# FFN 1's first projection as seven block products per pair of tiles, for tiles 8 to 15 of 18

## The chip, the cores and the metric

One core of one Trainium2 chip runs the whole program. The metric is the device time of one execution in microseconds (us). TensorE (PE) multiplies, VectorE (DVE), ScalarE (ACT) and GpSimd (POOL) do the elementwise work, SyncE (SP) issues nearly all DMAs. Only PE, DVE and ACT reach PSUM here, which has eight banks of 128 x 512 float32.

## The reference

Sliding-window attention with a linear bias, then two feed-forward networks (FFNs) on the same 2304 tokens of 512 numbers:

```python
scores = scale * q @ k.T + bias          # 4 batches, 8 heads, 576 positions, head size 64, window 128
x = softmax(scores) @ v                  # -> 2304 x 512
# FFN 1
h = x @ w_in                             # 512 -> 1024
solu = h * softmax(h)
ln = (solu - mean(solu)) / sqrt(var(solu) + 1e-6) * g_ln
x = ln @ w_out                           # 1024 -> 512
# FFN 2
g = x @ w_gate                           # 512 -> 1536
y = (silu(g) * (x @ w_val)) @ w_out2     # 1536 -> 512
```

## The kernel before

**Numbers.** PE works on a rounded 32-bit form (F32R). A float32 operand is split into a high and a low half (`high`, line 270, and `low`, line 276), and a product is taken as three matmuls, high x low, low x high and high x high (`HALVES`). The weights arrive as 64-bit words; `fetch` loads them and `unpack` (lines 311 to 319) turns them into float32 on ACT, DVE and POOL before they are split.

**Attention** goes in 20 steps (4 batches of five query tiles, the fifth half as long), each of four pairs of heads: `score` (line 463, matmuls on 32 x 64 pieces of the array), maximum and bias on DVE (499, 504), the exponential on ACT with the row sum as a second output (530, 539), then the transpose of the weights on PE (558), its copies out of PSUM (568 DVE, 571 ACT) and the product with v (607). In the first `SUMS` steps the division by the row sum is made after the product, with the inverted sums spread over a PSUM bank by matmuls (615, tile `rs` in SBUF holds the sums). In the later steps the sum goes to a PSUM bank, DVE inverts it (509, 510), and DVE, ACT or POOL divide (515, 517). The result is split into the halves of one token tile (128 tokens), in one of three places (`xs_at`).

**FFN 1** goes over 18 token tiles. `up(i)` is the first projection: two PSUM banks, 12 matmuls of 512 columns for each (line 712 in `pieces`), 24 for a tile; then maximum (735), exponential (746), product with h (748), variance (754), the power -0.5 on POOL (768) and the normalization (771). `flip(i)` transposes the tile, on PE (817) or, for tiles in `FLIP_BY_DMA`, by 16-bit halves through HBM (`pl`, 263 to 265, and `lscr`). `down1(i)` is the second projection, 24 matmuls of 512 columns, also at line 712, and its result goes to HBM (849).

**FFN 2** (`products`, line 1083; `steps_of`, line 1262) multiplies 2 x 2 blocks by seven products in place of eight (the Winograd form of Strassen's method): sums of blocks are made first (`seven`, line 982), and the products are added up in PSUM and on DVE.

**The order.** Each step is a generator that asks for slots (buffers, PSUM banks) and submits operations with a rank. The planner `Emitter.run` (line 199) keeps a clock for each engine with estimated costs, and emits, wherever an engine is free, the operation of the lowest rank that is ready; where an operation may go to several engines, the sum of end time and a bias (`B_DVE`, `B_ACT`) decides. So every constant at the head of the file moves instructions in all queues. At run time each engine executes its queue strictly in that order. A change between ordinary matmuls, those on 32 x 64 pieces (`form` 1) and those on 128 x 64 pieces (`form` 2) is counted by the planner at 95 ns, and `LEAST` and `PATIENCE` say how long such work is held back to be done together.

Of the kernel before, what the change touches and what calls it, by code (L numbers as in the profile page):

```python
# [35 lines left out]
PAIRS = (9, 29)  # L36
NTAIL = 2
DEC1 = (4, 2)
DEC2 = (2, 4)
RAW = 4  # L40
# [6 lines left out]
FLIP_BY_DMA = range(4, 14)  # L47
PLB = 2
SUMS = 4
PTB = 4  # L50
WHOLE = 20
VDB = 3
PW_2 = -0.766
LEAD = 3.373
R_FLIP = 0.741
R_DOWN = 3.0
PW_IN = [-0.63, -0.31, -0.37, -0.36, 0.17, 0.09, 0.35, 0.2]
PW_OUT = 5.23
B_DVE = 1863.684
B_ACT = 700.0  # L60
HALVES = [(0, 1), (1, 0), (0, 0)]
HB = NC2 // 2
O_MAX = 0.338
O_EXP = -0.005
O_INV = 0.814
O_TURN = -0.064
O_PT = -1.188
O_VAL = 0.0
O_X = 0.674
O_SC = 0.33  # L70
O_DEC = 0.0
O_SPL = -0.05
O_FLIP = -1.299
O_LN = -0.345
O_SET = 0.102
O_FREE = -1.17
# [3 lines left out]
PATIENCE = 517.289  # L80
LEAST = 3
# [27 lines left out]
class Emitter:  # L109
# [6 lines left out]
    def __init__(self):  # L116
        self.busy, self.pending, self.count, self.open = {}, [], 0, {}
        self.now = 0.0
        self.form = 0

# [77 lines left out]

    def run(self):
        while self.pending:  # L200
# [17 lines left out]
            if engine == "PE":  # L218
                if first > TOGETHER and getattr(fn, "form", 0) != self.form:
                    cost += 95.0  # L220
                self.form = getattr(fn, "form", 0)
            self.pending.remove(op)
# [9 lines left out]
def attention_then_two_ffns(ctx: ExitStack, tc: tile.TileContext, qk, v, w_in, w_out, g_ln, w2, tables_d, out):  # L232
# [28 lines left out]
    def halves_of(dst, src, n):  # L261
        words = src.bitcast(U16).rearrange("p (c h) -> p h c", h=2)
        return [(ACT, t_act(2 * n), lambda: nc.scalar.copy(dst, words)),
                (DVEP, t_dve(2 * n), lambda: nc.vector.tensor_copy(dst, words)),
                (POOL, 450.0 + 0.3 * 2 * n, lambda: nc.gpsimd.tensor_copy(dst, words))]
# [10 lines left out]
    def low(lo, src, hi, n, sbuf=True):  # L276
# [3 lines left out]
        return ways  # L280

# [202 lines left out]
    def attend(u):  # L484
# [34 lines left out]
        if c < SUMS:  # L519
            em.give(bank_s, ds[1], k)  # L520

            if pr == 0:
                yield rs_s
                rs[c] = at.tile([P, 3, 2 * NPAIR], F32, tag="rs", bufs=3, name="rs")
# [4 lines left out]
            for j, d in enumerate(ds):  # L529
                ex.append((yield (ACT, 93 + t_act(P, True, True), lambda j=j: nc.scalar.activation(  # L530
                    e[0:n, j], e[0:n, j], AF.Exp, bias=st[0:n, j:j + 1], scale=-1.0,
                    accum_out=rs[c][0:n, 0, 2 * pr + j:2 * pr + j + 1]), [d, ds[0]], 0.0, O_EXP)))
# [61 lines left out]
        if c < SUMS and pr == NPAIR - 1:  # L594
            for r in range(NPAIR):
                yield summed[c * NPAIR + r]
            y = yield (DVE, 160, lambda: nc.vector.tensor_scalar_add(rs[c][0:n, 1], rs[c][0:n, 0], 1e-9), (), 0.0, O_INV)
            inv.append((yield (DVE, 190, lambda: nc.vector.reciprocal(rs[c][0:n, 2], rs[c][0:n, 1]), [y], 0.0, O_INV)))
            sum_of[c] = yield bank_s

        def values():
# [9 lines left out]
            if inv:  # L611
                sums = banks[sum_of[c]].rearrange("p (r q) -> p r q", r=NPAIR)
                for r in range(NPAIR):
                    for j in range(2):
                        nc.tensor.matmul(sums[j * 64:(j + 1) * 64, r, 0:n], rs[c][0:n, 2, 2 * r + j:2 * r + j + 1].to_broadcast([n, 64]),
# [30 lines left out]
        while done < n:  # L646
            i, o = divmod(t0 + done, P)
            w = min(P - o, n - done)
            if i not in x_tiles:
                x_at[i] = yield x_s  # L650
                x_tiles[i] = xs_at[x_at[i]]
            hi, lo = (y[:, :, o:o + w] for y in x_tiles[i])
            src = src_x[:, :, done:done + w]
# [53 lines left out]

    def pieces(o, terms, per, cost):
# [7 lines left out]
    def up(i):  # L716
# [7 lines left out]
        (mx, mx2, sm, sm2, su, su2, nmu, nmu32, va, va2, s1, eps, var, rr) = (st[:, j:j + 1] for j in range(14))  # L724
# [18 lines left out]
        x = yield (DVE, 205, lambda: nc.vector.tensor_scalar(mx, mx, mx2, None, ALU.min), tops)  # L743
# [24 lines left out]
        x = yield (POOL, 470, lambda: nc.gpsimd.tensor_tensor(rr, var, mhalf, ALU.pow), [x])  # L768
# [122 lines left out]
    def fair(ways):  # L891
        return [(*w, 0.0) for w in ways]

    RG = NTT + LEAD + 2.4
    PROD = {"11": (0, 0), "22": (1, 1), "a4": (2, 5), "s3": (3, 6), "s1": (4, 4), "s2": (5, 3), "s4": (6, 2)}
# [7 lines left out]
    def second_region():  # L903
        for u in range(NU):
            yield started[u]
        yield valued[NS - 1]
        esa.close()
# [468 lines left out]
```

## Time and profile before

| | |
|---|---|
| median of 3 runs | 732.59 us (730.68 to 733.17) |
| the profiled execution | 732.14 us |
| its span, first to last instruction | 730.3 us |
| PE matmul, busy | 704.8 us (97%), 5148 matmuls |
| PE weight loads, busy | 635.2 us (87%) |
| DVE, ACT, POOL, busy | 540.0, 458.1, 272.2 us |

Times in the rows are in microseconds from the first instruction, unless marked ns. A matmul's end is modelled, and matmuls overlap, so the sum of their durations is longer than the time that they take in a row; the chain of waits gives that time, since in it a piece lasts until the next one begins. "PEld" is the loading of the stationary operand. L712 is line 712 of the kernel before.

### The profile page before, as it was taken

What the parts mean: (1) busy time and instruction counts of PE and PEld (TensorE: products, weight loads), DVE (VectorE), ACT (ScalarE), POOL (GpSimd) and SP (SyncE); (2) the same over time, 40 slices, a digit from 0 to 9 for tenths busy, and PEclk for the clock granted to TensorE, in tenths of its full rate; (3) what the DMA queues carried; (4) which work ended last, traced back from release to release, by engine and by line L of the source; (5) the groups of instructions that cost most, each with busy time, mean ns of one, the idle gap of its engine ahead of it and who ended that gap; (6) DMA issues with size and microseconds to landing.
All of it is one profiled execution on the core that took longest, in us unless ns stands there. A gap on an engine that the chain in (4) does not pass through costs nothing.

```text
span 730.3 us, 14535 instructions
## 1 busy us (share of the span) xinstructions
PE 704.8 (97%) x5148; PEld 635.2 (87%) x5148; DVE 540.0 (74%) x1480; ACT 458.1 (63%) x1127; POOL 272.2 (37%) x278
## 2 busy tenths in 40 slices
PE   5899899999999999999999999999999999999998
PEld 3567678777888888888899999999999999999997
DVE  6888985476566656988978767667775599886966
ACT  7899977777667775776647555655563574442532
POOL 3777776545675563550022412424221002110200
PEclk9999999999999999999999999999999999999999
DMA  8853325524454326256443454365541798886951
GB/s 289 249 168 109 103 73 146 167 89 116 133 151 109 94 75 173 73 145 148 150 170 131 151 169 163 125 188 190 184 151 66 263 360 307 254 299 203 300 177 66
DMA packets 92297, 121.86 MB, mean 167 GB/s; under 512 B 46400, under 2 KB 58688, under 8 KB 92224
## 3 DMA queue, kind: packets, MB, share of 16 engines
q1 hardware_dynamic: 91808, 120.48, 52.2%
q8 instruction: 40, 0.66, 0.4%
q10 hardware_dynamic: 416, 0.46, 0.2%
q14 instruction: 33, 0.27, 0.1%
HBM read 76.62 MB, written 34.34 MB: 152 GB/s over the span
## 4 chain that ended last, share of the span: by engine, by line
PE 76%; ACT 10%; DVE 9%; issue 2%; DMA 1%; POOL 1%; ACTq 0%; SPq 0%; DVEq 0%; POOLq 0%
PE bank L1083 31%; PE bank L712 21%; PE bank L1262 18%; PE bank L607 2%; ACT e L539 2%; PE bank L463 2%; PE bank L558 2%; ACT bank L754 1%; ACT pt L571 1%; ACT e L530 1%; DVE e L504 1%; PE bank L817 1%; DVE yt L277 1%; DMA tables<-tables 1%; DVE pt L568 1%
## 5 line engine op out<-in xcount | busy, mean ns | idle before, releaser
L1083 PE MATMUL bank<-yt,w 128*128 128x384 f32 x1008 | 186.3, 337 | 1.8 <-ACT t L1112 1.0
L1083 PEld LDWEIGHTS bank<-yt,w 128*128 128x128 f32 x1008 | 176.2, 188 | 4.1 <-ACT set L1110 1.5
L1262 PE MATMUL bank<-w,wo 128*128 128x384 f32 x756 | 133.1, 337 | 0.6 <-DVE set L1123 0.6
L319 POOL TENSOR_TENSOR db<-db,dw 128x512 int32<-128x512 int32 x52 | 73.2, 1409 | 161.2 <-DVE db L317 110.7
L1262 PEld LDWEIGHTS bank<-w,wo 128*128 128x128 f32 x756 | 132.4, 188 | 0.9 <-DVE set L1123 0.9
L712 PE MATMUL bank<-wout,lnT 128*128 128x512 f32 x432 | 102.5, 392 | 0.0
L1083 PE MATMUL bank<-shared,w 128*128 128x384 f32 x504 | 97.6, 337 | 0.0
L712 PEld LDWEIGHTS bank<-wout,lnT 128*128 128x128 f32 x432 | 80.4, 188 | 16.7 <-issue 0.2
L1083 PEld LDWEIGHTS bank<-shared,w 128*128 128x128 f32 x504 | 88.2, 188 | 1.1 <-ACT set L1110 0.5
L712 PE MATMUL bank<-shared,shared 128*128 128x512 f32 x288 | 79.8, 410 | 0.8 <-ACT shared L273 0.8
L712 PEld LDWEIGHTS bank<-shared,shared 128*128 128x128 f32 x288 | 52.2, 191 | 13.0 <-issue 1.9
L539 ACT ACTIVATE e<-e,st 128x128 f32<-128x128 f32 (+1 forms) x128 | 49.7, 402 | 21.5 <-DVE st L504 19.8
L273 ACT CAST w<-t 128x384 fp32r<-128x384 f32 (+2 forms) x35 | 26.6, 771 | 39.7 <-DVE t L1206 27.4
L504 DVE CUSTOM_DVE_ANT_0 e<-bank,bias 128x128 f32<-128x128 f32 (+1 forms) x160 | 38.2, 283 | 6.9 <-PE bank L463 5.0
L517 POOL TENSOR_TENSOR e<-e,st 128x256 f32<-128x256 f32 (+1 forms) x55 | 33.2, 618 | 21.9 <-ACT e L539 9.9
L277 DVE TENSOR_TENSOR w<-db,w 128x512 fp32r<-128x512 f32 (+1 forms) x46 | 31.4, 690 | 12.7 <-ACT w L273 12.4
L311 ACT ACTIVATE dw<-dw 128x512 int32<-128x512 uint32 x52 | 35.0, 675 | 7.0 <-DMA dw<-w 5.1
L316 DVE TENSOR_SCALAR db<-db 128x512 uint32<-128x512 uint32 x52 | 27.5, 532 | 16.0 <-ACT db L315 16.0
L273 ACT CAST w<-db 128x512 fp32r<-128x512 f32 (+1 forms) x48 | 26.9, 566 | 19.7 <-POOL db L319 9.4
L317 DVE SCALAR_TENSOR_TENSOR db<-dw,db 128x512 uint32<-128x512 uint32 x52 | 38.5, 744 | 0.8
L712 PE MATMUL bank<-shared 128*128 128x512 f32 x144 | 39.1, 394 | 0.0
L558 PE MATMUL bank<-tables,e 128*128 128x128 f32 x160 | 29.7, 293 | 9.0 <-ACT e L530 5.8
(124 smaller groups left out, 1242.7 us busy)
## 6 DMA issues: line engine op xcount, KB each, us to landing
dw<-w SPq DMA_DIRECT2D x36, 512.0 KB, 4.1
t<-ascr SPq DMA_DIRECT2D x21, 768.0 KB, 6.0
ascr<-set SPq DMA_DIRECT2D x34, 384.0 KB, 2.7
later<-ascr SPq DMA_DIRECT2D x15, 768.0 KB, 5.9
wo<-wscr SPq DMA_DIRECT2D x6, 896.0 KB, 7.2
v<-v SPq DMA_DIRECT2D x20, 256.0 KB, 3.6
lscr<-pl SPq DMA_DIRECT2D x20, 256.0 KB, 2.4
raw<-qk SPq DMA_DIRECT2D x19, 256.0 KB, 4.0
```

The source lines that it names most:

```text
L273: return [(ACT, t_act(n, sbuf), lambda: nc.scalar.copy(hi, src)), (DVEP if sbuf else DVE, t_dve(n, sbuf), lambda: nc.vector.tensor_copy(hi ...
L277: ways = [(DVEP if sbuf else DVE, t_dve(n), lambda: nc.vector.tensor_sub(lo, src, hi.bitcast(F32)))]
L311: r = yield (ACT, t_act(512), lambda: nc.scalar.activation(a, lw, AF.Copy, scale=2.0 ** -29), (), 0.0, O_DEC)
L317: x = yield (DVEP, t_dve(512), lambda: nc.vector.scalar_tensor_tensor(b, hw, 0x80000000, b, ALU.bitwise_and, ALU.bitwise_or), [x], 0.0, O_DEC)
L319: x = yield (POOL, t_pool(512), lambda: nc.gpsimd.tensor_tensor(b.bitcast(I32), b.bitcast(I32), a, ALU.add), [x, r], 0.0, O_DEC)
L504: d = yield (DVE, t_dve(P), lambda j=j: nc.vector.tensor_tensor_reduce(e[0:n, j], sc[0:n, j * 256:j * 256 + P], bias[0:n, 2 * pr + j, bs], ...
L517: eng.tensor_tensor(e[0:n], e[0:n], st[0:n, 6:8].unsqueeze(2).to_broadcast([n, 2, P]), ALU.mult)
L539: ex.append((yield (ACT, 93 + t_act(P, True, True), lambda j=j: nc.scalar.activation(e[0:n, j], e[0:n, j], AF.Exp, bias=st[0:n, j:j + 1], ...
L558: nc.tensor.transpose(tp[:, j], e[:, j], ident)
L712: nc.tensor.matmul(o, terms[m][0], terms[m][1], start=(m == 0), stop=(m == len(terms) - 1))
L1083: nc.tensor.matmul(o, l, r, start=first and m == 0, stop=m == 5, skip_group_check=True)
L1262: nc.tensor.matmul(o, w[:, b], ob[k, i][a][:, j], start=i == 0 and m == 0, stop=i == HB - 1 and m == 2)
```

## The change

For tiles 8 to 15 the first projection of FFN 1 is made two tiles at a time (`UPP`), by seven products of 2 x 2 blocks for eight. The two rows of blocks are the two tiles; the 512 inner numbers and the 1024 columns are halved. Each product is six matmuls of 512 columns: 42 for a pair, where two tiles took 48.

- `sums_of_w` makes four sums of blocks of `w_in` once, after the last weight of `w_out` has been decoded, and puts them into the buffers of the decoder (`dw`, `db`), into `rec`, and into one new tile (`sums`).
- The attention result of these tiles is copied to `xf` as float32, not split. One `xf` holds a pair, and there is one (`XF`).
- `combine` makes the block sums of the pair with `seven` and splits them into `xc` (one set).
- `up_pair` issues the seven products (line 876 of the changed kernel) in four banks: 11, 22, s1, s2, s4, s3, a4. A bank is added to again after it has been copied out: s2 waits for the copy of 11, s4 for that of s1, s3 for that of s2 (ACT, line 881), a4 for a DVE sum.
- The row sums of the first `SUMS` steps go to a PSUM bank (taken at the start of the step) in place of SBUF; `SUMS` is 5 for 4.
- The planner counts slow stretches of PE's clock (`paced`, with `WARM` and `COOL`), and nearly all its constants have new values. Tile 3 is transposed through HBM too, and there are three `raw` tiles for four and one `pl` for two.

The diff, cut to its core:

```diff
+UPP = range(8, 16, 2)
+XF = 1
-RAW = 4
+RAW = 3
-FLIP_BY_DMA = range(4, 14)
-PLB = 2
-SUMS = 4
+FLIP_BY_DMA = range(3, 14)
+PLB = 1
+SUMS = 5
-LEAD = 3.373
-R_FLIP = 0.741
+LEAD = 3.281
+R_FLIP = 0.274
-B_DVE = 1863.684
-B_ACT = 700.0
+B_DVE = 1575.488
+B_ACT = 554.749
...
-PATIENCE = 517.289
-LEAST = 3
+PATIENCE = 134.638
+LEAST = 4
+WARM, COOL = 3400.0, 1900.0
...
+    def paced(self, t, cost):
+        gap = t - self.warmed
+        if gap > COOL:
+            self.rest = WARM
+        elif self.rest and gap > 400.0:
+            self.rest = WARM
+        slow = min(2 * cost, self.rest)
+        self.rest -= slow
+        cost += slow / 2
+        self.warmed = t + cost
+        return cost
...
-                    accum_out=rs[c][0:n, 0, 2 * pr + j:2 * pr + j + 1]), [d, ds[0]], 0.0, O_EXP)))
+                    accum_out=banks[sum_of[c]][0:n, 2 * pr + j:2 * pr + j + 1]), [d, ds[0]], 0.0, O_EXP)))
...
+    def up_pair(i):
...
+        kd = yield bank_s
+        x1 = yield from product(kd, "11", first=True)
+        c1 = yield (*copied(ei[:, 0], kd, x1)[0], *copied(ei[:, 0], kd, x1)[1:])
+        kx = yield bank_s
+        x2 = yield from product(kx, "22", first=True)
+        a1 = yield summed_(banks[kx], ei[:, 0], kx, tops[0][0], [x2, c1])
+        kb = yield bank_s
+        x5 = yield from product(kb, "s1", first=True)
+        c5 = yield (*copied(ej[:, 0], kb, x5)[0], *copied(ej[:, 0], kb, x5)[1:])
+        x6 = yield from product(kd, "s2", [c1])
+        u2 = yield (*copied(ei[:, 1], kd, x6)[0], *copied(ei[:, 1], kd, x6)[1:])
+        x3 = yield from product(kb, "s4", [c5])
+        a2 = yield summed_(banks[kb], ei[:, 1], kb, tops[0][1], [x3, u2])
+        em.start(soft(i, ei, sts[0], [kx, kb], [a1, a2], 2), i + LEAD)
+        x7 = yield from product(kd, "s3", [u2])
+        kz = yield bank_s
+        a3 = yield summed_(banks[kz], ej[:, 0], kd, tops[1][1], [x7, c5])
+        x4 = yield from product(kd, "a4", [a3])
+        a4 = yield (DVE, t_dve(512), lambda: nc.vector.reduce_max(tops[1][0], banks[kd], axis=AX.X), [x4])
+        em.give(xc_s, x4)
+        em.start(soft(i + 1, ej, sts[1], [kd, kz], [a4, a3], 2), i + 1 + LEAD)
...
+    em.start(sums_of_w(), R_T + LEAD)
     for i in range(NTT):
-        em.start(up(i), i + LEAD)
+        if i in UPP:
+            em.start(up_pair(i), i + LEAD)
+        elif i - 1 not in UPP:
+            em.start(up(i), i + LEAD)
```

Two places show how instructions move. On PE, before, the first projection of a tile stands in long runs. This is the end of tile 9 (`shared` holds `w_in` and x, `lnT` is the normalized and transposed tile of `down1`, `tables,e` is a transpose in attention):

```order
L712 MATMUL bank_83<-shared_73,shared_74 128x512 x2
L712 MATMUL bank_83<-shared_73 128x512 x4
L712 MATMUL bank_84<-shared_74,shared_73 128x512 x4
L712 MATMUL bank_84<-shared_73,shared_74 128x512 x4
L712 MATMUL bank_84<-shared_73 128x512 x4
L712 MATMUL bank_82<-wout_76,lnT_2293 128x512 x8
L712 MATMUL bank_82<-wout_75,lnT_2294 128x512 x8
L712 MATMUL bank_82<-wout_75,lnT_2293 128x512 x8
L558 MATMUL bank_80<-tables,e 128x128 x2
```

In the change, for the pair of tiles 12 and 13, the end of product s1 (bank 81), then s2 (bank 79), two transposes, s4 (bank 81 again) and s3 (bank 79 again) stand so:

```order
L876 MATMUL bank_81<-dw,xc_2126 128x512 x2
L876 MATMUL bank_79<-dw,xc_2126 128x512 x2
L876 MATMUL bank_79<-dw,xc_2127 128x512 x2
L876 MATMUL bank_79<-dw,xc_2126 128x512 x2
L580 MATMUL bank_86<-tables,e 128x128 x2
L580 MATMUL bank_83<-tables,e 128x128 x2
L876 MATMUL bank_81<-shared_74,xc_2126 128x512 x2
L876 MATMUL bank_81<-shared_73,xc_2127 128x512 x2
L876 MATMUL bank_81<-shared_73,xc_2126 128x512 x2
L876 MATMUL bank_79<-sums,xc_2126 128x512 x2
L876 MATMUL bank_79<-sums,xc_2127 128x512 x2
L876 MATMUL bank_79<-sums,xc_2126 128x512 x2
```

Where no bank was used twice by one tile, banks 81 and 79 now come back one product and two transposes later, with a copy in between on another engine.

On ACT, before, the work of an attention step stands together in the middle stretch. Here are exponentials (539), the cast of an attention result (273), two divisions (515), and the exponential of FFN 1 (746):

```order
L539 ACTIVATE e,bank_83<-e,st 128x128
L273 CAST shared_73<-bank_79 128x4x64
L539 ACTIVATE e,bank_83<-e,st 128x128
L539 ACTIVATE e,bank_86<-e,st 128x128 x2
L539 ACTIVATE e,bank_85<-e,st 128x128 x2
L515 ACTIVATE e<-e,st 128x128 x2
L273 CAST shared_73<-bank_79 128x4x64
L746 ACTIVATE e_3422,mst<-bank_84,mst 128x512
```

In the change, at the pair of tiles 12 and 13, the copies of s1 (bank 81) and s2 (bank 79) stand between exponentials of attention (561):

```order
L561 ACTIVATE e,bank_86<-e,st 128x128 x2
L561 ACTIVATE e,bank_83<-e,st 128x128 x2
L561 ACTIVATE e,bank_82<-e,st 128x128
L881 COPY e_3122<-bank_81 128x512
L561 ACTIVATE e,bank_82<-e,st 128x128
L561 ACTIVATE e,bank_84<-e,st 128x128
L881 COPY e_3000<-bank_79 128x512
L593 COPY pt<-bank_86 128x256
```

Five exponentials, each behind its DVE maximum, stand ahead of the copy for which s4 waits, and two more ahead of the one for which s3 waits.

## Rows read from the trace of the kernel before

**Rows 1.** Busy time by stretch: length, PE, PEld, DVE, ACT, POOL, PEclk (granted TensorE clock).

```profile
0.00:20.00 20.00, 11.10 (x144) 6.81 (x152) 12.27 (x49) 15.43 (x45) 8.66 (x12) 1.00 0.84 285
20.00:40.00 20.00, 16.64 (x257) 11.31 (x239) 17.31 (x80) 17.32 (x62) 14.97 (x12) 0.91 0.82 255
40.00:60.00 20.00, 18.64 (x194) 14.07 (x193) 16.59 (x62) 16.71 (x55) 13.28 (x13) 1.00 0.41 131
60.00:80.00 20.00, 19.23 (x220) 14.59 (x220) 17.23 (x72) 19.86 (x61) 17.20 (x20) 1.00 0.37 115
80.00:100.00 20.00, 17.73 (x185) 13.87 (x183) 16.91 (x75) 16.97 (x55) 15.26 (x18) 0.91 0.26 79
100.00:120.00 20.00, 18.53 (x159) 14.71 (x141) 15.79 (x64) 16.15 (x47) 15.12 (x17) 1.00 0.33 87
...
120.00:280.00 160.00, 158.54 (x1540) 126.72 (x1539) 95.70 (x465) 108.90 (x359) 89.77 (x106) 1.00 0.45 124
```

**Rows 2.** Chain that ended last, one period of the middle stretch: start, length, what.

```profile
244.33 1.02 PE bank L607 x16
245.36 9.77 PE bank L712 x42
255.12 0.87 PE bank L558 x8
255.99 1.40 PE bank L712 x6
257.39 1.02 PE bank L607 x16
258.41 1.22 PE bank L463 x32
259.63 1.02 PE bank L607 x16
260.66 9.79 PE bank L712 x42
```

**Rows 3.** The same chain: single pieces from 32 to 320 us.

```profile
32.87 0.87 PE bank L615 x16
...
127.65 1.02 PE bank L817 x8
...
137.06 0.71 PE bank L463 x32
...
212.20 0.59 PE bank L607 x8
212.79 1.27 PE bank L463 x64
...
314.68 5.46 PE bank L712 x24
320.15 1.05 PE bank L1083 x6
```

**Rows 4.** DMA issues: KB each, median us from issue to landing.

```profile
lscr<-pl SPq DMA_DIRECT2D x20, 256.0 KB, 2.4
e<-lscr SPq DMA_TRANSPOSE x20, 3.6
```

**Rows 5.** Waits of SP's queue, whole span: us in total, times, longest.

```profile
SPq L258 <- DMA lscr<-pl: 13.0, 10, 4.0
```

**Rows 6.** Instructions by line and shape: busy us, mean ns of one, idle before and releasers.

```profile
L277 DVE TENSOR_TENSOR w<-db,w 128x512 fp32r<-128x512 f32 x36 | 27.2, 765 | 2.5 <-ACT w L273 2.1
L273 ACT CAST w<-db 128x512 fp32r<-128x512 f32 x36 | 22.1, 620 | 14.2 <-DVE db L993 7.2 <-POOL db L319 3.9 <-POOL db L994 3.0
L273 ACT CAST lnT<-bank 128x512 fp32r<-128x512 f32 x16 | 9.0, 595 | 0.0
L277 DVE TENSOR_TENSOR shared<-bank,shared 128x256 fp32r<-128x256 f32 x20 | 8.3, 421 | 3.7 <-ACT shared L273 3.6
L273 ACT CAST shared<-bank 128x256 fp32r<-128x256 f32 x20 | 7.4, 386 | 3.4 <-PE bank L607 2.1 <-PE bank L712 1.2
L539 ACT ACTIVATE e<-e,st 128x128 f32<-128x128 f32 x96 | 37.5, 404 | 14.6 <-DVE st L504 13.3
L539 ACT ACTIVATION_READ_ACCUMULATOR e<-e,st 128x1 f32 x96 | 15.5, 161 | 0.0
```

**Rows 7.** Weight loads of line 712: busy us, mean ns.

```profile
L712 PEld LDWEIGHTS bank<-wout,lnT 128*128 128x128 f32 x432 | 80.4, 188 | 16.7 <-issue 0.2
```

**Rows 8.** Waits of ACT, 120 to 280 us: us in total, times, longest.

```profile
ACT e L539 <- DVE st L504: 18.3, 11, 2.7
```

**Rows 9.** Waits of PE weight loads for ACT copies in FFN 2, whole span.

```profile
PEld bank L1083 <- ACT set L1110: 1.9, 5, 0.7
```

**Rows 10.** Matmuls of `down1`: ns (min, median, max), first and last start.

```profile
L712 PE MATMUL bank<-wout,lnT x432: 387/389/504, 111.2 to 326.2; 128*128 128x512 f32 x144
```

More of the change, by code (lines that the diff above doesn't have):

```diff
@@ new lines, in combine, with put @@
+    def combine(i):
+        a, b = (x_tiles[j][0].rearrange("p k c -> p (k c)") for j in (i, i + 1))
+        yield x_done[i]
+        xa = Done(em.now)
+        yield x_done[i + 1]
+        xb = Done(em.now)
+        yield xc_s
+        def put(o, src, n, deps):
+            hi, lo = (t[:, o:o + n // 256].rearrange("p j c -> p (j c)") for t in combos())
+            x = yield (high(hi, src, n), deps, 0.0, O_T)
+            x = yield (fair(low(lo, src, hi, n)), [x], 0.0, O_T)
+            return x
+        xs = yield from seven(a, xa, b, xb, put)
+        for x, d in zip(xs, c_ok[i]):
+            chain(x, d)
+        for x in xs:
+            yield x
+        em.give(xf_s, max(xs, key=lambda x: x.time))
@@ new lines, in up_pair, with weights, product, f @@
+    def up_pair(i):
+        if i:
+            yield upped[i - 1]
+        for _ in range(2):
+            yield h_s
+        es_ = []
+        for j in (i, i + 1):
+            yield e1_s
+            es[j] = m1.tile([P, 2, 512], F32, tag="e1", bufs=E1, name="e1")
+            es_.append(es[j])
+        ei, ej = es_
+        sts = [m1.tile([P, 14], F32, tag="mst", bufs=4, name="mst") for _ in range(2)]
+        part = {"11": 0, "22": 0, "a4": 1, "s3": 2, "s1": 2, "s2": 3, "s4": 3}
+        def weights(j):
+            if j in (0, 1, 2):
+                r, cs = ((0, 0), (2, 0), (2, 1))[j]
+                return [[win[c][:, r + k, cs * 512:cs * 512 + 512] for k in range(2)] for c in range(2)]
+            return tw[{3: 0, 4: 1, 5: 2, 6: 3}[j]]
+        def product(k, name, deps=(), first=False):
+            p, j = PROD[name]
+            yield c_ok[i][part[name]]
+            for n in range(2):
+                yield t_ok[{3: 0, 4: 1, 5: 2, 6: 3}[j]][n] if j > 2 else free_now
+            for d in deps:
+                yield d
+            w = weights(j)
+            x = combos()
+            o = banks[k]
+            def f():
+                for m, (a, c, r) in enumerate([(a, c, r) for a, c in HALVES for r in range(2)]):
+                    nc.tensor.matmul(o, x[a][:, p, r * P:(r + 1) * P], w[c][r], start=first and m == 0, stop=m == 5,
+                                     skip_group_check=True)
+            return (yield (PE, 6 * 233.0, f))
+        def copied(dst, k, dep):
+            return (ACT, t_act(512, False), lambda: nc.scalar.copy(dst, banks[k])), [dep], 0.0, O_UC
+        def summed_(o, a, k, top, deps):
+            return (DVE, 80 + t_dve(512), lambda: nc.vector.tensor_tensor_reduce(
+                o, a, banks[k], 1.0, -3.0e38, ALU.add, ALU.max, top), deps, 0.0, O_UC)
+        tops = [[t[:, 0:1], t[:, 1:2]] for t in sts]
+        kd = yield bank_s
[19 more added lines that the diff above has]
+        em.start(soft(i + 1, ej, sts[1], [kd, kz], [a4, a3], 2), i + 1 + LEAD)
+        yield x4
+        for j in (i, i + 1):
+            upped[j].settle(x4.time)
```

167 lines of the change are left out of this document (132 added, 35 removed).

## The prediction

> **What bounds the kernel now.** I read the busy time by stretches first, then the chain of waits, then the durations by line, and the waits last.
>
> The stretches split the program in three. Up to 120 us PE is held up by others: in 20 to 120 us it is busy for 90.8 of 100 us, while ACT is busy for 87.0 and DVE for 83.8 (sums of the five rows). In two of these slices the granted clock is 0.91, so PE ran part of them at 1.2 GHz: 9% of 20 us, 1.8 us each [rows 1]. From 120 to 280 us PE is busy for 158.5 of 160 us, at the full clock; ACT has 51 us to spare there (160 - 108.9) and DVE 64 (160 - 95.7). FFN 1's tiles 8 to 15 lie mostly in this stretch.
>
> The chain confirms it. One period takes 15.3 us (245.36 to 260.66) and every piece of it is PE: one tile's 24 + 24 matmuls of 512 columns, four pairs of transposes, scores, and products with v [rows 2]. Nothing else is on the path there. So a matmul removed in this stretch is worth its own spacing, provided that no wait takes its place. After it FFN 2 follows, whose PE order the change leaves almost alone; PE is the bound there too, so time gained earlier stays gained.
>
> **The change part by part**, against the profiled execution (732.1 us; the median of the runs is 0.5 us longer).
>
> *Products.* Four pairs take 42 matmuls for 48: 24 fewer, of 512 columns. 24 such in a row last 5.46 us in the chain [rows 3]: **-5.5 us**, all in the stretch where PE is the bound.
>
> *Transposes of tile 3* go from PE to a DMA: eight matmuls, one piece of 1.02 us at 127.65 us, on the chain [rows 3]: **-1.0**. What comes instead are two copies to `pl`, two stores (2.4 us to landing) and two transposing DMAs (3.6), which stand in SP's queue ahead of loads for attention; SP has waited 4.0 us at the longest for such a store [rows 4, 5]. With one `pl` the halves go one after the other, and with three `raw` tiles a load is asked for one step later. I count nothing for these, since other FFN work covers them on PE; without that cover one late load costs up to 4 us, once.
>
> *Row sums of a fifth step.* Sixteen more spreading matmuls, on a half-length tile; for a full one a piece of 16 lasts 0.87 us [rows 3]. Between half of it and all of it, I take **+0.6**. In return DVE, ACT and POOL lose the inversions and divisions of one step, off PE's path. The sums in PSUM hold a bank for the length of a step, in the first five steps only, where ACT and DVE set the pace and not the banks: nothing.
>
> *Smaller pieces.* Scores and products with v stand in 62 runs on PE before and in 72 after. A run of 64 scores lasts 1.27 us, one of 32 lasts 0.71; 16 products with v last 1.02 us, eight last 0.59 [rows 2, 3]. (The 32 scores of 1.22 us belong to a half-length step, which has fewer pieces of the array to work on at once.) So cutting a run in two costs 2 x 0.71 - 1.27 = 0.15, or 2 x 0.59 - 1.02 = 0.16 us. Ten more: **+1.6**, at the least 0.8, since five of them lie ahead of the first `down1`, where PE waits anyway.
>
> *Sums of the weights and of x.* DVE gets 24 operations of 512 for the weights (16 sums, 8 low halves) and for x 12 low halves of 512, 3 of 256 and 15 sums of 256; ACT gets 20 casts of 512 and 4 of 256. A low half of 512 takes 765 ns, one of 256 takes 421, a cast 620 and 386 [rows 6]: DVE 36 x 0.765 + 18 x 0.42 = 35 us, ACT 20 x 0.62 + 4 x 0.39 = 14 us. ACT also gets 12 copies of products (595 ns each, 7 us) and copies x to `xf` in place of the casts. DVE saves the low halves of x for these tiles (421 ns for 256, some 7 us). DVE's 12 sums that also give a maximum stand for 12 maxima. Net: DVE +28, ACT +21 us, spread over the 160 us in which they have 64 and 51 us free [rows 1, 6]. I count **0**: the idle time hides it. If the cover fails, the products wait; that is the first rival.
>
> *The new order in the early stretch.* New constants move all queues. Ahead of the first result of `down1` ACT has 90 exponentials and divisions for 74, some of them taken from POOL; the PE order there is much like before. From the rows it can gain the 9.2 us in which PE is not busy from 20 to 120 us and the 3.6 us of slow clock, or lose as much if ACT, already busy for 19.86 of 20 us in one slice, fills up [rows 1]. The planner now counts slow stretches, which makes a gain likelier than a loss, but nothing in the trace tells how much. I take **0** and keep -6 and +6, about half of it, as ends.
>
> Sum: -5.5 - 1.0 + 0.6 + 1.6 = -4.3. 732.1 - 4.3 = **727.8 us**.
>
> **A rule against it.** In the middle stretch the weight loads are busy for 126.7 of 160 us, 79%, where the matmul rows show 99% [rows 1]. The Trainium skill (Perfetto Trace Analysis, Identifying the Most-Contended Engine) says that matmul busy time is no good measure of how near PE is to its limit, and that the busy share of weight loads is one. By that rule a fifth of PE's time would be slack and removing matmuls need not shorten anything. The rows speak for the matmuls: in an unbroken run of 24 in 5.46 us the 24 loads of 188 ns fill 4.5 us, 83%, so about 80% is what 512-column matmuls show when PE is full [rows 3, 7]. By the one the sum would be 732, by the other it is 727.8.
>
> **The rivals.**
>
> *A product waits for its copy (slower).* In each pair s4 can start only after ACT has copied s1, and s3 only after s2 has been copied. At tiles 12 and 13 PE has one product (1.4 us) and two pairs of transposes (0.44) between, and on ACT five exponentials stand ahead of the first copy and two ahead of the second. ACT waits for DVE's maximum ahead of such exponentials for 1.7 us on average (18.3 / 11), 2.7 at the longest [rows 8]. One such wait in front of a copy and one copy left bare (0.6) come to 2.3 us a pair, 9.2 in all: 737 us. Slower begins at 734.8 by the runs, 734.3 on the scale of the profiled execution, so it decides when a pair loses more than (734.3 - 727.8) / 4 = 1.6 us. Against it: FFN 2 has the same pattern 36 times, and weight loads waited 1.9 us in all for the copy of line 1110 [rows 9]. For it: there ACT and DVE have no attention between.
>
> *ACT fills up early (no change).* The 16 operations more on ACT ahead of the first `down1` cost 0.40 us each, an exponential with the reading of its sum 0.57: 6.4 to 9.1 us, against the 13 us in which ACT is idle from 20 to 120 us [rows 1, 6]. If half of them cannot be fitted into that idle time, the first `down1` comes some 4 us later and the gain is eaten: 732 us.
>
> *Slack on PE (no change).* PE's matmuls in the middle stretch are not its limit; removing some only widens gaps, and the path runs through ACT and DVE: 732 us. Against it: the chain shows nothing but PE for a whole period [rows 2]. The rule above says this.
>
> *A larger gain.* The new order also takes half of the early waits and one slow stretch away: 0.5 x 9.2 + 1.8 = 6.4 us more: 721.4 us. For it: nearly every constant was set anew together with the count of slow stretches. Against it: the early stretch is bound by ACT and DVE, and their work there isn't less.
>
> **How the numbers follow.** About 0.3%, 2.2 us, is what a measurement here can tell from no change. The forecast (724.5 to 730) gets 0.47, the larger gain 0.15, ACT full early 0.13, slack on PE 0.04, the slower rival 0.21. Hence faster 0.62, same 0.17, slower 0.21. The range reaches down to 720.5, which holds the larger gain but for a tail of 0.05, and up to 736.5, which leaves out about half of the slower rival.
>
> **What would show it.** Right: 192 matmuls of 512 columns of FFN 1 become 168, still 0.227 us apart; the first `down1` starts near 111 us as before [rows 10]; PE stays busy for 99% between 120 us and the last pair; the first FFN 2 product comes some 4 us or more ahead of 320 us [rows 3], and the time from there to the end is as before. Wrong: waits of PE at line 876 for ACT's line 881 above 1 us a pair (first rival); a `down1(0)` that starts more than 3 us later, or a third slice with a granted clock under 1.00 (no change); early PE busy time well above 91 of 100 us (larger gain). A gain that is there when FFN 2 begins and is lost by the end would be a case that I have not counted.

## The result and the profile after

The changed kernel takes **742.49 us** (median of 5 runs, 741.96 to 743.74), against 732.59 us before: ratio of the means 1.0146, with a 95% interval of 1.0129 to 1.0163. It is slower by 1.5%, where the forecast was 0.6% faster, and lies above the range (736.5). The profiled execution after has a span of 740.6 us.

These are the rows of after that answer to [rows 1]: busy time by stretch (length, PE, PEld, DVE, ACT, POOL, granted clock), with three stretches more.

```profile
0.00:20.00 20.00, 11.08 (x136) 6.51 (x136) 14.00 (x55) 15.24 (x45) 8.45 (x11) 1.00 0.80 275
20.00:40.00 20.00, 18.14 (x260) 12.45 (x260) 13.43 (x55) 16.11 (x53) 12.54 (x11) 1.00 0.65 211
40.00:60.00 20.00, 16.43 (x214) 11.54 (x210) 15.67 (x75) 18.01 (x61) 14.08 (x11) 1.00 0.49 156
60.00:80.00 20.00, 19.03 (x205) 14.35 (x203) 15.18 (x65) 19.04 (x61) 13.81 (x16) 1.00 0.37 124
80.00:100.00 20.00, 18.21 (x190) 13.46 (x188) 18.07 (x77) 18.88 (x58) 13.89 (x15) 1.00 0.24 73
100.00:120.00 20.00, 18.98 (x158) 13.59 (x157) 17.24 (x75) 18.20 (x62) 15.24 (x18) 1.00 0.40 106
...
120.00:140.00 20.00, 18.59 (x155) 14.40 (x154) 19.64 (x55) 14.98 (x41) 8.98 (x8) 1.00 0.27 80
...
120.00:280.00 160.00, 153.38 (x1444) 116.57 (x1443) 118.39 (x493) 129.88 (x397) 92.88 (x100) 1.00 0.46 125
...
155.00:285.00 130.00, 124.56 (x1157) 94.05 (x1155) 94.02 (x401) 107.30 (x329) 71.66 (x82) 1.00 0.46 122
...
340.00:360.00 20.00, 19.19 (x99) 18.53 (x100) 15.74 (x28) 12.04 (x24) 0.00 (x0) 0.91 0.68 172
```

DVE is up by 22.7 us and ACT by 21.0 from 120 to 280 us, about what the forecast had worked out (28 and 21), and both still look far from full. Yet PE is busy for 153.4 of the 160 us, where it was 158.5. The granted clock of the early slices is better than before (no slice under 1.00), and yet time is lost there, as the table below shows.

The chain of waits says more. First the same view of the kernel before over 200 to 285 us (shares of the stretch by engine and line), then the kernel after over the same time:

```profile
by line: PE bank L712 78.8%; PE bank L607 10.3%; PE bank L463 5.9%; PE bank L558 5.1%
32 pieces in order of time: start us, us, what
```

```profile
by line: PE bank L876 15.0%; PE bank L917 9.7%; ACT e L561 7.5%; issue 6.6%; DVE e L961 5.4%; ACT bank L967 5.1%; DVE xc L295 4.7%; PE bank L580 4.4%; ACT lnT L291 3.9%; ACT pl L281 3.3%; ACT e L959 3.2%; ACT ys L1062 3.1%; ACT e L881 2.3%;
217 pieces in order of time: start us, us, what
...
211.58 1.40 PE bank L876 x6
213.01 0.70 DVE bank L884
214.02 0.69 ACT e L536 x2
214.71 0.67 ACT e L959 x2
215.38 0.26 ACT pt L593
215.64 0.69 ACT e L959 x2
216.36 0.71 DVE e L961 x2
...
217.34 1.53 ACT bank L967 x4
219.08 0.75 DVE bank L520 x2
219.83 1.36 DVE e L961 x4
...
224.20 0.60 POOL mst L981
224.89 0.62 POOL e L538
225.56 0.44 PE bank L580 x2
```

Before, 32 pieces, every one of them PE. After, 217 short pieces over all engines, and behind one product (line 876) the path leaves PE for 12.6 us (212.98 to 225.56; PE goes on working, but off the path): it goes through the pair's sum (line 884), then down the queues of ACT and DVE, where the tile's own exponentials, products and squares (lines 959, 961, 967) and the attention's share the order, and comes back over POOL's division of the probabilities (line 538) to a transpose (line 580). No engine is full in this stretch; PE has ceased to be what decides.

PE's waits from 155 to 285 us (us in total, times, longest), first of the kernel before, then after, show the same place. After, the waits are at the attention's transposes, hardly at the products:

```profile
PE bank L558 <- ACT e L515: 0.5, 1, 0.5
PE bank L607 <- ACT pt L571: 0.2, 1, 0.2
```

```profile
PE bank L580 <- POOL e L538: 1.8, 4, 0.9
PE bank L580 <- DVE shared L295: 1.0, 1, 1.0
PE bank L580 <- ACT xf L691: 0.7, 1, 0.7
PE bank L580 <- ACT pt L593: 0.6, 2, 0.3
...
PE bank L876 <- DVE mst L884: 0.2, 1, 0.2
```

Matmuls of `down1`, answering to [rows 10]: the first starts at 117.2 us, 6.0 later than before, and the last 10.2 later.

```profile
L917 PE MATMUL bank<-wout,lnT x432: 387/390/505, 117.2 to 336.4; 128*128 128x512 f32 x144
```

**Where the time went.** To compare kernels in different orders I add up, at each moment, the PE work that is still to come (each kind of matmul at its undisturbed spacing, an estimate from the traces), and read at which time a kernel has the same work left. A table of this, worked out from the matmul records, in us against the kernel before (minus is ahead). Kernels with 24 matmuls fewer are 5.4 us ahead from the start by this count, so the changed kernel is to be read against the line "24 fewer", the first experiment below; the other lines are the kernels of experiments 2 and 4 to 6. One profile stands behind each line. The kernels "24 fewer", "fewer buffers", "urgency O_TURN" and "other B_DVE" have PE's order of before up to 130 us at least, and yet are 1.2 to 1.7 us further ahead at 113 us than at 64 us: the profile of before has a slice at 0.91 from 80 to 100 us and theirs have not. So about 1.5 us of a difference to the kernel before says nothing of the order.

```
work left, us       640    600    560    500    440    350    200
before is there at 64.1  113.2  155.8  218.1  279.0  372.6  524.1
24 fewer           -5.3   -6.5   -7.1   -5.6   -4.6   -4.6   -4.7
after              -2.4   -3.6   -1.8   +3.7   +8.0  +10.2  +10.2
small sums         -2.3   -3.3   -1.6   +4.7   +7.0   +9.6   +9.5
no pairs           +4.7   +3.9   +4.7   +5.2   +7.8   +8.7   +8.6
products alone     -5.2   -6.6   +1.5   +6.3  +14.9  +18.0  +18.2
 sums on POOL      -5.8   -7.1   -4.7   +1.6   +8.8  +10.7  +10.9
 small, planned    -5.5   -5.2   +3.0   +7.3  +13.5  +15.3  +15.1
count alone        -1.0   +5.4   +6.7   +5.8   +5.7   +5.8   +5.7
PSUM sums alone    +0.1   +3.5   +4.9   +4.4   +4.3   +4.3   +4.3
costs alone        -0.5   +1.7   +2.6   +2.7   +4.4   +5.7   +5.6
urgency O_TURN     +0.5   -1.1   -0.5   +1.8   +4.8   +5.8   +5.7
urgency LEAD       -0.8   +3.4   +5.2   +4.6   +4.6   +4.6   +4.6
fewer buffers      +0.6   -1.1   -1.2   -0.4   -0.4   -0.4   -0.4
other B_DVE        +0.1   -1.5   -1.6   -1.5   -1.5   -1.2   -1.8
```

After against 24 fewer: 5.3 us lost by 156 us, 7.3 between 156 and 279, 2.2 between 279 and 373, nothing later. That is 14.8, of which the saved matmuls give back 4.6: +10.2, as measured (+9.9 by the medians). The kernel without pairs loses 4.7 us by 156 us, but also 3.1 between 156 and 279, so not all of the 7.3 can be put down to the pairs. The 2.2 us stand around FFN 2's beginning, where PE waits 1.8 us for ACT's line 1320 and 0.8 for POOL's line 984 (the normalization of a last FFN 1 tile), and one slice has a clock of 0.91. The last column is not the end for all: "no pairs" loses 2.7 us more after 524 us, "PSUM sums alone" and "urgency O_TURN" 1.7 each.

### The profile page after: what moved, and what is told of

Read it like the earlier page. It is cut to its first block, busy times and chain, and to the rows that moved or that the text cites. A ratio compares the mean times of both kernels' runs of the same rounds, so it can differ in the third digit from the quotient of the medians.

```text
span 740.6 us, 14583 instructions
## 1 busy us (share of the span) xinstructions
PE 708.4 (96%) x5132; PEld 629.0 (85%) x5132; DVE 566.5 (76%) x1521; ACT 489.2 (66%) x1193; POOL 277.3 (37%) x267
## 4 chain that ended last, share of the span: by engine, by line
PE 58%; DVE 17%; ACT 14%; issue 4%; DMA 4%; POOL 2%; SPq 0%; ACTq 0%; DVEq 0%; POOLq 0%
PE bank L1293 28%; PE bank L1472 17%; PE bank L917 6%; PE bank L876 3%; ACT e L561 2%; ACT bank L967 1%; DVE yt L295 1%; PE bank L580 1%; DVE e L961 1%; ACT e L959 1%; DVE db L338 1%; DVE t L1245 1%; PE bank L484 1%; DVE pt L590 1%; ACT lnT L291 1%
## 5 line engine op out<-in xcount | busy, mean ns | idle before, releaser
L917 PE MATMUL bank<-wout,lnT 128*128 128x512 f32 x432 | 106.5, 397 | 1.4 <-DVE pt L590 1.4
L561 ACT ACTIVATE e<-e,st 128x128 f32<-128x128 f32 (+1 forms) x120 | 47.4, 402 | 7.6 <-DVE st L525 6.2
L580 PE MATMUL bank<-tables,e 128*128 128x128 f32 x160 | 34.9, 301 | 13.2 <-ACT e L552 4.0
L580 PEld LDWEIGHTS bank<-tables,e 128*128 128x128 f32 x160 | 19.8, 144 | 31.8 <-ACT e L552 8.0
L917 PE MATMUL bank<-shared,shared 128*128 128x512 f32 x160 | 44.4, 410 | 0.4 <-ACT shared L291 0.3
L484 PE MATMUL bank<-keys,raw 64*32 64x160 f32 (+1 forms) x1152 | 34.6, 323 | 8.3 <-DMA raw<-qk 5.1
L295 DVE TENSOR_TENSOR w<-db,w 128x512 fp32r<-128x512 f32 (+1 forms) x46 | 33.3, 734 | 10.8 <-ACT w L291 10.7
L1327 ACT ACTIVATE set<-set 128x384 f32<-128x384 f32 x34 | 17.7, 525 | 32.8 <-DVE set L1325 32.6
L295 DVE TENSOR_TENSOR w<-t,w 128x384 fp32r<-128x384 f32 (+2 forms) x35 | 30.4, 872 | 9.5 <-ACT w L291 9.5
```

The costliest lines, as they stand in the source:

```text
L295: ways = [(DVEP if sbuf else DVE, t_dve(n), lambda: nc.vector.tensor_sub(lo, src, hi.bitcast(F32)))]
L484: nc.tensor.matmul(banks[ks[r]][i:i + Q, o:o + w], raw[c][rows, 2 * qd + j, i:i + Q], kt[rows, 2 * qd + j, k0:k0 + w], start=True, stop=True)
L580: nc.tensor.transpose(tp[:, j], e[:, j], ident)
L917: nc.tensor.matmul(o, terms[m][0], terms[m][1], start=(m == 0), stop=(m == len(terms) - 1))
```

## The experiments

Ratios are against the kernel before on the same chip (its medians were 731.1 to 732.1 us).

**1. What are 24 matmuls worth?** The kernel before, its order untouched; tiles 8 to 15 leave out 3 of 24.

```
- for m in range(k, k + per):
+ for m in range(k, k + per):
+     if m in out_of: continue      # out_of: (4, 6) and (4,)
```

> The kernel before, with three of the 24 first-projection matmuls of each of the tiles 8 to 15 left out (24 in all, so part of FFN 1's first projection is not computed); the order is that of before. If a matmul of this stretch is worth its own spacing, as the prediction says: 732.6 - 5.5 = 727 us (726 to 728.5). If PE has slack there and others set the pace: 731 to 733 us.

728.63 us, ratio 0.996 [0.9945, 0.9975]: 2.7 us less by the medians, just outside the 726 to 728.5 that were expected. In the profile it is 4.6 us ahead at 279 us, of the 5.5 that the matmuls last, and keeps it to 620 us, where 0.9 go. PE is still what the chain of 200 to 285 us runs through:

```profile
by line: PE bank L714 75.7%; PE bank L607 10.1%; PE bank L463 6.5%; PE bank L558 4.1%; ACT pt L571 1.2%; PE bank L820 1.0%; ACT bank L757 0.8%; DVE pt L568 0.4%; DVE mst L766 0.3%; issue 0.1%
```

So the step "24 matmuls less in the middle are worth their spacing" is right in mechanism, and in size 2.7 (medians) to 4.6 (one profile) for 5.5.

**2. The change without its pairs; with the old constants; with small sums.**

```
no pairs:   - UPP = range(8, 16, 2)   + UPP = ()    (and no sums of weights)
constants:  - new values   + the values of before, but for RAW and PLB
small sums: tiles 10 to 15: sums and splits over 16 columns (the others left out), order kept
```

> The changed kernel with no pairs (all 18 tiles by eight products), all its other constants and the row sums in PSUM kept; the planner makes a new order. Theory load (what the pairs add on ACT and DVE delays the attention chain, and PE waits for it): back at 730 to 734 us. Theory constants (the new values make a poorer order, with or without pairs): 739 us or more.

> The changed kernel with pairs, but with all the constants of before except three raw tiles and one pl tile, which the space for the pairs demands. Theory load: 738 us or more. Theory constants: 727 to 733 us. A third theory, that the single pl tile makes the transposes by DMA late, also gives 738 or more here and has to be told apart in another run.

> The changed kernel in its own order; for tiles 10 to 15 the block sums of x and their splits work on 16 columns in place of 256 or 512 (so the products of these tiles use wrong sums). That takes some 12 us of work from DVE and 6 us from ACT, and no instruction. Theory load: 735 to 738.5 us. Theory constants, or the single pl tile: 741 to 743 us.

Without pairs: 742.55 us, 1.0149 [1.0127, 1.0172], as slow as with them. With pairs and old constants: 749.62, 1.0254 [1.0234, 1.0273]. With small sums: 739.39, 1.0114 [1.0093, 1.0136], between the two ranges that were expected. DVE is relieved of 5.9 us between 155 and 285 us, half of what was meant (94.02 before the edit):

```profile
155.00:285.00 130.00, 125.96 (x1162) 96.17 (x1162) 88.11 (x406) 103.97 (x331) 69.85 (x83) 0.99 0.48 124
```

So two losses lie on top of each other: one that is there without the pairs, and one that the pairs bring and that the length of their sums explains only in part.

**3. Is the first loss the buffers?** No pairs, with the old or new constants and 3 or 4 `raw` tiles (RAW), 1 or 2 `pl` tiles (PLB).

```
old constants, RAW 4, PLB 2 | old, RAW 3, PLB 1 | new, RAW 4, PLB 2 | new, RAW 3, PLB 2
```

> The changed kernel's code with no pairs and with every constant of before (four raw tiles, two pl tiles): against before only the row sums in PSUM and the planner's count of slow stretches are left, with a few of its costs. If these two lose the time: 738 us or more. If the buffers or the constants lose it: 730 to 733 us.

> The same with three raw tiles and one pl tile. Theory buffers (the space that the pairs take from raw and pl is what costs): 737 us or more, and the run with four and two 730 to 733. Theory constants, or row sums: no more than 1 us from the run with four and two.

> The changed kernel with no pairs, all its new constants, but four raw tiles and two pl tiles. Theory buffers: 730 to 735 us, against 742.6 with three and one. Theory constants: 740 us or more.

> The changed kernel with no pairs, all its new constants, three raw tiles, but two pl tiles. If the single pl is the buffer that costs: within 2 us of the run with four and two. If the third raw tile is: within 2 us of 742.6. Theory constants: 740 us or more in both.

744.62 us (1.0181 [1.0161, 1.02]), 739.33 (1.0105 [1.0086, 1.0125]), 742.22 (1.0145 [1.0121, 1.0169]), 740.63 (1.0122 [1.0107, 1.0137]). More buffers are no faster, and neither set of constants is needed for the loss. What all four share is the sums in PSUM, the planner's count and its costs, and all lose 7 to 13 us.

Three times now a kernel with pairs can be set beside one that differs in the pairs alone (with what belongs to them): the changed kernel and "no pairs" (ratios 1.0146 and 1.0149), the one with old constants and RAW 3, PLB 1 (1.0254 and 1.0105), and, from experiment 5, the products alone and fewer buffers (1.0243 and 1.0012). The pairs cost nothing, 11 and 17 us net (estimates from the ratios): what they cost depends on the plan into which they are put.

**4. Which of these three?** Each alone on the kernel before; and as a control another value of one constant.

```
count:   + cost = self.paced(t, cost)
PSUM:    - accum_out=rs[c][...]        + accum_out=banks[sum_of[c]][...]
costs:   - 450.0 + 0.3 * 2 * n, 470    + 980.0, 580
control: - B_DVE = 1863.684            + B_DVE = 1850.0
```

> The kernel before with one thing of the change alone: the planner's count of half-clock stretches on TensorE (WARM 3400, COOL 1900, `paced`); the instructions are the same kind and number, only their order is planned anew. If this count is what orders the early stretch badly, the time rises by most of what the change lost: 738 to 744 us, with 3 to 6 us already lost at 70 us of the span. If the row sums in PSUM are the cause, 731 to 734. If any new plan of this finely set order costs some us, 735 to 742, and then the kernel with the slightly different constant costs about as much.

> The kernel before with the row sums of the softmax in PSUM alone: a bank is taken at a step's first pair and held until the step's sums are spread over the partitions, costs and constants unchanged. If the bank held early starves the scores and transposes of the first steps, 737 to 743 us, with 3 to 6 us lost at 70 us of the span and longer waits for a bank there. If the planner's count or its costs are the cause, 731 to 734 us. If any new plan costs some us, 735 to 742.

> The kernel before with the two changed GpSimd costs of the planner alone (the copy of halves 980 ns at any size, the power 580 ns); nothing that a kernel executes is changed but the order. If these costs are the cause, 737 to 743 us. If the sums in PSUM or the count of half-clock stretches are, 731 to 734 us. If any new plan costs some us, 735 to 742.

> The kernel before with the planner's allowance for VectorE, B_DVE, at 1850 ns for 1863.7: no part of the change, only another order of the same instructions from some point on. If the old order is a finely set one and any other costs time, 735 to 742 us; if the loss comes from a part of the change, 731 to 734 us.

737.45 us (1.0088 [1.0071, 1.0105]), 736.93 (1.0075 [1.0058, 1.0092]), 738.37 (1.0098 [1.0083, 1.0114]); the control 731.62 (1.0006 [0.9996, 1.0017]). Three parts that share nothing cost about the same, 5.9 to 7.3 us each, and not in one place: by the table between 64 and 113 us (count), up to 156 us and again after 524 us (sums), in small steps up to 373 us (costs). None had lost, by 70 us, the 3 to 6 us that two of the expectations named. The control came out as the expectation had it for "a part of the change", but its instructions keep the order of before up to 293 us on every engine, so it could not speak for the early order.

**5. Any other early order, and the products alone.**

```
- O_TURN = -0.064  + O_TURN = -0.2      (r1)
- LEAD = 3.373     + LEAD = 3.3         (r2)
- RAW, PLB = 4, 2  + RAW, PLB = 3, 1    (q0)
q1: q0 and the pairs; row sums in SBUF, no count, old costs
```

> The kernel before with one urgency of the planner changed, O_TURN (the transposes of the probabilities) from -0.064 to -0.2: no part of the change, the same instructions, another order from the second step on. If the old order is a finely set one and almost any other plan of the early stretch costs time, 735 to 742 us, lost before 170 us. If the parts of the change are what costs time, 731 to 734 us.

> The kernel before with LEAD 3.3 for 3.373 alone, the rank at which FFN 1's tiles stand against the steps: no part of the change, another order from the first step on. If almost any other plan of the early stretch costs time, 735 to 742 us; if the parts of the change do, 731 to 734 us.

> The control of the kernel with the products alone: the kernel before with RAW 3 and PLB 1 and nothing else. If a new plan of the early stretch costs time, or the buffers do, 735 to 742 us; if the parts of the change are what costs, 731 to 734 us.

> The products of pairs with the buffers that they leave (RAW 3, PLB 1) and the old constants, but the row sums in SBUF, no count of half-clock stretches and the old costs. If the stretch of the pairs itself loses time, whatever the early order is, it ends 742 to 750 us and loses 5 us or more against the kernel with three of 24 matmuls left out between 155 and 285 us at equal remaining work. If the rest of the change is what costs, 727 to 733 us.

O_TURN 739.08 us (1.0099 [1.0074, 1.0124]), LEAD 737.45 (1.0077 [1.0055, 1.0099]), fewer buffers 731.92 (1.0012 [0.9996, 1.0027]), products alone **750.02** (1.0243 [1.0216, 1.0269]).

One urgency moved alone costs as much as any part of the change, although it adds no work. (The expectations call the two urgencies no part of the change; the changed kernel moves both the same way, and further: O_TURN to -0.536, LEAD to 3.281.) With one thing moved, five plans (count, sums, costs, two urgencies) cost 5.9 to 7.6 us each by their medians; two did not, the one with fewer buffers and the late control. In the traces, the four that move PE's order before 113 us (LEAD from 35 us, the sums 35, the count 16, the costs 71) have all lost 2.6 to 6.7 us by 156 us; O_TURN moves it only from 131 us on and loses its time after 156 us, and fewer buffers, from 164 us on, lose nothing. So "lost before 170 us" held for LEAD, not for O_TURN: there is no one place. That the order of before is a finely set point fits all this; that any other order costs as much is not shown, since all seven go a step towards the change. How such a loss looks: PE's longest wait between 86 and 109 us with the count alone, and PE's only waits between 200 and 290 us with O_TURN.

```profile
PE bank L478 <- ACT bank L769: 3.4, 1, 3.4
```

```profile
PE bank L558 <- POOL e L517: 1.1, 3, 0.5
```

Each time a matmul waits for an operand or a bank whose last step is another engine's. With the count the clock has a part in it as well: from 86 to 109 us it averages 0.78.

```profile
86.00:109.00 23.00, 16.82 (x180) 11.99 (x180) 17.50 (x74) 19.97 (x64) 20.06 (x19) 0.78 0.13 37
```

The products alone keep PE's old order up to 134 us (-6.6 us at 113 us, as the kernel with 24 fewer), and show the second loss by itself: 6.6 us while the work left falls from 590 to 580 us, then 15 more to 294 us. The first part can be read outright: PE's instructions (start, length, engine, line; the wait in brackets), then DVE's in that time, then the busy time in slices of 5 us.

```profile
127.26 0.66 PE L1029 MATMUL bank<-ident,e 128*128 128x128 f32 x4
132.66 1.11 PE L1029 MATMUL bank<-ident,e 128*128 128x128 f32 x4 [4.74 <-DVE lnT L294]
133.44 7.77 PE L916 MATMUL bank<-wout,lnT 128*128 128x512 f32 x23
```

```profile
128.30 0.69 DVE L294 TENSOR_TENSOR sums<-pl,sums 128x512 fp32r<-128x512 f32 x1
128.91 0.68 DVE L758 TENSOR_TENSOR xf<-xf,pl 128x512 f32<-128x512 f32 x1
129.51 0.68 DVE L294 TENSOR_TENSOR dw<-xf,dw 128x512 fp32r<-128x512 f32 x1
130.11 0.68 DVE L758 TENSOR_TENSOR pl<-shared,xf 128x512 f32<-128x512 f32 x1
130.72 0.68 DVE L294 TENSOR_TENSOR dw<-xf,dw 128x512 fp32r<-128x512 f32 x1
131.32 0.68 DVE L758 TENSOR_TENSOR pl<-pl,shared 128x512 f32<-128x512 f32 x1
131.92 0.68 DVE L294 TENSOR_TENSOR lnT<-bank,lnT 128x512 fp32r<-128x512 f32 x1
```

```profile
125.00:130.00 5.00, 2.92 (x54) 2.19 (x52) 5.00 (x11) 3.45 (x10) 0.00 (x0) 1.00 0.65 201
130.00:135.00 5.00, 2.34 (x8) 1.98 (x9) 4.51 (x11) 2.17 (x6) 1.04 (x1) 0.65 0.02 9
135.00:140.00 5.00, 5.00 (x17) 3.93 (x16) 3.94 (x29) 3.88 (x16) 2.73 (x4) 0.67 0.39 107
```

The low half `lnT`, for which PE waits, stands behind a row of weight sums and their splits; the first product that uses one starts at 175 us. PE idles for 4.74 us. From 130 to 140 us the granted clock averages 0.65 and 0.67, so PE ran at 1.2 GHz for a part of that time: 23 matmuls take 7.77 us, for 5.2 at the spacing of [rows 3] (5.46 / 24). POOL is busy for 1.0 us from 125 to 135 us.

**6. The two losses of the pairs.** On the products alone: the weights' sums on POOL; and, in another kernel, small sums for tiles 10 to 15 that the planner knows of.

```
p2: - fair([(DVEP, ...), (POOL, ...)])   + [(POOL, ...)]
p1: - 512 and 256 columns, t_dve(256)    + 16 columns, t_dve(16)
```

> The kernel with the products alone, with the sums and differences of the weights on GpSimd, which is idle for 15.5 us there, instead of VectorE. If the 6.6 us lost at 117 to 127 us are TensorE waiting for a split of down1's operand that stands behind these sums in VectorE's queue, they go: 742 to 745 us. If GpSimd's queue then holds up what the attention waits for, or the place of the sums does not matter, 748 us or more.

> The kernel with the products alone, with the sums and splits of tiles 10 to 15 on 16 columns (so the products of these tiles are of wrong sums) and their small cost known to the planner, which plans anew from the second pair on, some 200 us. The order before that is the old one. If the load of these sums on VectorE, ScalarE and GpSimd loses the time, the 8.7 us that the kernel with the products alone loses between 207 and 290 us fall to 3 or less: 742 to 745 us. If the products, their copies and their banks among the attention steps lose it, 747 to 751 us.

Sums on POOL: 743.79 us, 1.0159 [1.0133, 1.0186]. That loss goes (-5.6 for +0.1 us with 580 us left), although such a sum takes 1.28 us on POOL for 0.68 on DVE. A part of the gain is lost again at another place: from 560 to 540 us left this kernel loses 5.9 us, the products alone 1.3 (by the same count, between the columns of the table). There PE stops for 3.1 us for a division on ACT (line 535); it stands in ACT's queue behind a split that had waited 2.6 us for a tile transposed through HBM, with 6 us of ACT's work between, and the clock is at 0.66 from 160 to 170 us. Whether this follows from the sums' new place is not shown.

```profile
PE bank L578 <- ACT e L535: 3.1, 1, 3.1
```

```profile
ACT lnT L290 <- DMA e<-lscr: 2.6, 1, 2.6
```

```profile
160.00:165.00 5.00, 2.98 (x37) 1.88 (x38) 3.10 (x17) 4.45 (x13) 3.64 (x4) 0.66 0.77 205
165.00:170.00 5.00, 5.00 (x16) 3.97 (x15) 3.54 (x20) 4.66 (x17) 3.06 (x4) 0.66 0.43 104
```

It ends far behind the kernel before, since the later loss stays as well. Small sums, planned: 747.39, 1.022 [1.02, 1.0241]. From 500 to 440 us left it loses 6.2 us for 8.6, with 9.5 us less on DVE from 200 to 285 us: the load of these sums is about 2.4 of 8.6, and the theory that they are what loses the time falls. (The products' copies and their sums out of PSUM were not made smaller.) PE's chain from 200 to 285 us is broken as before the edit:

```profile
by line: PE bank L918 15.2%; PE bank L877 12.0%; ACT e L559 9.1%; issue 6.7%; PE bank L627 5.1%; ACT bank L968 4.5%; DVE e L962 4.2%; PE bank L483 3.9%; ACT e L960 3.7%; DVE e L524 3.7%; DVE xc L294 3.7%; ACT pt L591 3.3%; PE bank L578 3.2%
```

Stops of PE, counted in the matmul records from 155 to 285 us (a gap over 0.15 us beyond the spacing of the kind), and changes from one kind of matmul to another:

```
                  stops   us   changes
before              11    2.9    63
24 fewer            15    4.5    63
urgency LEAD        11    2.4    66
no pairs            19    5.6    80
after               27   10.6   100
small sums          28    9.8   100
products alone      30   12.3    96
 small, planned     26   10.4    93
 sums on POOL       38   14.2    77
```

Two rows hold matmuls that were only slow: small sums has a clock of 0.66 from 160 to 165 us, sums on POOL from 160 to 170.

In the kernel before, one period of attention and FFN fits one tile, and repeats. A pair is two tiles with one set of buffers and banks, its seven products come in pieces between the attention's transposes, and the regular period is gone; a part of that is there without pairs too (80 changes for 63). The stops grow by 7.7 us against before and by 6.1 against 24 fewer, more than the 5.5 that the products save; against the kernel without pairs they grow by 5.0, about what the products save. That the lost period is what makes the stops is argued from these counts, not shown.

What of it is the pair's four banks and what the copies and sums of its products that stand in ACT's and DVE's queues, the runs don't tell apart: no kernel with fewer banks for a pair was tried. No version that does the whole computation is faster than the kernel before.

## Why the prediction was wrong

The mechanism that it rested on, PE as the bound of the middle stretch, was true of the kernel before and ended with the change. Two terms of its sum that were put at 0 failed.

- *Products*, -5.5: the matmuls are worth 2.7 to 4.6 as long as the order stays (experiment 1). The 168 that were forecast are there; in the changed kernel their worth was outweighed.
- *Sums of the weights and of x*: "I count 0: the idle time hides it." **This step failed.** DVE's +22.7 and ACT's +21.0 us are near the 28 and 21 of the forecast, and the idle time was there, but idle time counted over 160 us is no cover in queues that run in order: what matters is what stands ahead of the operand that PE needs next. The products alone show one such place whole (4.74 us and the clock behind it). In the changed kernel the stretch of the pairs costs 7.3 us; 3.1 are lost there without pairs too, so 4.2 are the pairs' share if the two add up, which no run shows. That agrees with the times: with or without pairs 742.5 us, so they lose about what their products save. By experiment 6 the length of the sums is the smaller part of it; what the rest is stays open.
- *The new order in the early stretch*: "I take 0." **This step failed too**, and it is the larger one, since the kernel without pairs is as slow as the changed one (1.0149). By 156 us it is +5.3 us, near the end of -6 to +6 that was kept for it; the order moves later as well, which the term left out. "The planner now counts slow stretches, which makes a gain likelier than a loss" was a guess, and the count alone costs 6.4 us. The clock did improve as hoped. What I lacked was the price of another order as such: 5.9 to 7.6 us in five of seven cases, each with one step of the change alone.
- *Time gained earlier stays gained*: 2.2 us more were lost where FFN 2 begins, where PE waits for lines 1320 and 984 and the clock falls once; after 373 us it holds.
- *Transposes of tile 3*, *row sums of a fifth step*, *smaller pieces* (-1.0, +0.6, +1.6): not measured alone. The pieces were seen, but taken for a fixed cost each; the counts of experiment 6 make them rather the sign of a lost period.
- *A product waits for its copy* did not happen in the changed kernel: 0.2 us in all at line 876. In the products alone it did, 1.4 us. The forecast's slower rival had the right sign and the wrong place, so it was right by luck.
- *ACT fills up early* was close for its stretch: it said a first `down1` some 4 us later; it came 6.0 later, with ACT busy for 90.2 of 100 us (87.0 before, sums of the rows from 20 to 120 us). It was priced as no change because the products were to pay for it. That ACT's load is what delays it, no run shows.
- *Slack on PE* is refuted by experiment 1: with PE's order kept, leaving out 5.5 us of matmuls shortened the time by 2.7 us (medians) and brought the profiled program 4.6 us ahead up to 620 us. The rule of the Trainium skill (Perfetto Trace Analysis, Identifying the Most-Contended Engine) that the weight loads' busy share tells how full PE is would have called a fifth of that stretch slack; here the measurement differs and decides (79% weight loads, 99% matmuls).
- *Signs named beforehand*: "a `down1(0)` that starts more than 3 us later" came, as did PE at 96% for 99% from 120 us on; the first FFN 2 product came at 321.7, not 316 us, and FFN 1's last products follow it up to 336.4 us.

## What to carry to other kernels

A matmul taken out of a stretch that PE bounds is worth its spacing only while PE stays the bound; before counting on idle time of the other engines, ask of each added operation which operand of PE's stands behind it in the same queue. Where a planner sets the whole order, measure first what a plan with one constant moved and no work added costs: here 6 to 7.6 us for two urgencies, more than the gain that was sought, and nothing for two that leave the early order alone. So a part that re-plans everything must be judged against such a control, or with the order kept.

## What was not expected of the hardware

In the kernel with the products alone PE waited for 4.74 us (127.9 to 132.7), and from 130 to 140 us the mean granted clock was 0.65 to 0.67; 23 matmuls took 2.5 us longer there than at the full clock, so the wait cost half as much again as its length. And the early clock is not a thing of PE's order alone: four kernels with PE's order of before have 1.00 from 80 to 100 us, where the profile of before has 0.91.
